# A two-layer transformer kernel on one core: loads by whole rows, Q and K in banks of their own, and a new order of the products

## The chip, the cores and the metric

The kernel runs on one core of a Trainium2 chip. A core has a matrix engine (TensorE, in the profile PE, with PEld for its weight loads), three engines for other arithmetic (VectorE or DVE, ScalarE or ACT, GpSimd or POOL) and a queue engine (SyncE or SP) that issues DMA transfers. TensorE reads its operands from the on-chip memory SBUF and writes into PSUM, here eight banks of 128 partitions by 512 float32; DVE and ACT copy ("evict") results out of a bank before it is used again.

The metric is the device time of one execution in microseconds (us): the median of 3 runs.

## The reference, cut to what matters

The computation is attention with a recurrent memory (A), then a gated feed-forward network (B), and both again with the same weights:

```python
# x: 2048 x 576; 32 heads of 128; 8 memory rows; segments of 32 rows
def A(x, mem0, Wq, Wk, Wv, Wo):
    mem = mem0
    for s in range(64):
        xs = x[32 * s:32 * s + 32]
        h = concat(mem, xs)                      # 40 rows
        q, k, v = h @ Wq, h @ Wk, h @ Wv         # per head
        p = softmax(masked(q @ k.T * 128 ** -0.5))
        o = sum over heads of (p @ v) @ Wo
        mem, out_s = o[:8], o[8:]                # memory goes to the next segment
def B(x, w1, w3, w2):                            # 576 -> 4608 -> 576
    return (silu(x @ w1) * (x @ w3)) @ w2

x = x + A(layernorm(x)); x = x + B(layernorm(x))
x = x + A(layernorm(x)); x = x + B(layernorm(x))
```

(Written out in short form; inputs are bfloat16.) The memory makes the 64 segments of a layer a chain. The kernel therefore walks 72 steps: step t does segment t of the first layer and segment t - 8 of the second one together, where both exist. 576 is 4 x 128 + 64, so every product over Dm has four blocks of 128 rows and a remainder of 64 rows.

## The kernel before: the parts concerned

The kernel builds a list of nodes (a block of products, an eviction, a load), and places them with a small planner. The order of TensorE's nodes is not planned: it is given as a string of letters.

```python
KINDS = {"m0tr": "m", "L0tr": "a", "L1tr": "b", "POST": "p", "Ftr": "n", "QK": "Q", "QKt": "q", "SC": "S", "TR": "T", "PV": "P",
         "WO": "O", "WOt": "o", "VX": "X", "VXt": "x", "VM": "V", "VMt": "v", "FF": "F", "FFt": "f", "VG": "G", "VGt": "g", "W2": "W", "W2b": "w"}
...
ORDER = FIRST + FOUR * 11 + LAST
```

Q is a block of QK products for four heads, q its 64-row remainder; S scores, T the transposed product of the softmax, P its product with V, O and o the products with Wo, X, V and G the V products (small letters their remainders), F, f, W and w the feed-forward network. FOUR is the order of four steps, repeated eleven times.

The loads of the input weights, all on the SP queue:

```python
    def load_qk(self, half):
        def f(n):
            for kind, wd in ((0, self.a.wq), (1, self.a.wk)):
                for c in range(4):
                    w, d = (v.rearrange("p (r h n) -> p r h n", r=2, h=2)[:, :, half] for v in (self.T.W[:, 4 * kind + c, :], wd[c * P:(c + 1) * P, :]))
                    self.dma(w, d)
...
    def load_qkt(self):
        def f(n):
            for kind, wd in ((0, self.a.wq), (1, self.a.wk)):
                self.dma(self.T.W[:, 8, kind * 2048:(kind + 1) * 2048], wd[4 * P:D, :].rearrange("p (r n) -> r p n", r=2))
...
    def load_vt(self):
        return lambda n: self.dma(self.wv(True), self.a.wv[4 * P:D, :].rearrange("p (r n) -> r p n", r=2))
```

A remainder is folded: its 64 rows fill partitions 0 to 63 with the first half of the heads and partitions 64 to 127 with the second, so that two products of 64 rows run side by side in the two halves of the array (the "row" tiling mode).

The QK block and its remainder for unit u (four heads), into two banks:

```python
            for j in range(4):
                h0 = self.head(u // 2, 4 * (u % 2) + j) * E
                for kind in (0, 1):
                    at = (2 * kind + j % 2) * SW
                    for c in range(4):
                        self.mm(self.bk(b[j // 2])[:, at:at + q1 - q0], self.T.W[:, 4 * kind + c, h0:h0 + E], HTt[:, c, q0:q1],
                                first and j % 2 == 0 and kind == 0 and c == 0, c == 3)
...
            for i in (0, 1):
                for kind in (0, 1):
                    at = (2 * kind + i) * SW
                    h0 = (H // 2 * kind + 2 * u + i) * E
                    for r in (0, 1):
                        rr = slice(r * R64, (r + 1) * R64)
                        self.mm(self.bk(b[r])[:, at:at + q1 - q0], self.T.W[rr, 8, h0:h0 + E], HTt[rr, 4, q0:q1],
                                first and i == 0 and kind == 0, True, tile_position=(r * R64, 0))
```

Bank b[0] holds Q and K of the first two heads, b[1] those of the other two. Each bank is evicted by one node, in two copies where both layers are present.

The products with Wo accumulate in a bank that is set apart (YB), while all others come from a pool of seven. After the last Wo product of a step, four small nodes carry the result on: an ACT copy of the new memory columns into HT, an ACT copy of the odd part (YO), a DVE addition for the memory's remainder, and the copies for the residual (YTS).

Of the kernel before, what the change touches and what calls it, by code (L numbers as in the profile page):

```python
# [13 lines left out]
P = 128  # L14
R64 = 64
# [20 lines left out]
POOLS = {"bank": 7, "y": 1, "qkt": 4, "sme": 2, "pb": 2, "pts": 1, "ot": 4,  # L36
# [148 lines left out]
def ewh(*ns):  # L185
# [5 lines left out]
    "amQQqqqqSqQQqSqQQQTQqSSXxvVPTPTOPOTOoooPOoQqqqQQSqqqQQSQQTSVqvqPTQOPSoTOXPToxPOOooaQqqqQQSqQVvSqqQQQqSQqTSPTPOTO"  # L191
    "PTOPoooOoQQqqVSqqvQQQSqQqqqQSTQPTSXPOTOPTxooPOOooQqqqpQvqSVQnQFfqSQQFqqfQQfqSTFSPWTFPOoTOPfoTFPOOooWQfqqQQSqqQQS"
    "qfqQFTFfvVWSQqPQTFqffFSxPOTWPXfFTOPOOooooWQFqqfQFSfqqQQQSqqWTQQFqfvVSqfQFFPSfTWPOTOafPFTOPFOoooofWQQqqvfqSFVQWQq"
    "QSqqQTQPqqSQbOTSXxPXTOPTooPOOooxQQpqqVSqqvQnQQFSfqFTfqQPQqqfSFQTOPSWTOPFOTFPffoooOoWQQqqqQSgqfFQGWQTqSPQFqfqQQSq"
    "fFGTFggfSGPOTOPGfgTOPFOooooWQqqqQQFSffqFaQWQQSqqqQqfFTQWvSVFPTfSOPFfTOPfWOTFPFOooooWQqqfQQSfqqFQWQQqqSqqQbQTGggS"
    "PGTGPSggOTGPOTOPoooOoQqqvppQQSqVqqnQnQFTSfqPQQfqqSFTQPOfoSFOTWwPFffTFPOOooowFfqQWQFqffFWSqQwQgqqGTQSPQqqfFQWGTQg"
    "qSOPFSogfGwTOPFgfGaTOPWOoooFQqqfQwQSqqVqvQQQSfqqQTFPFfqSQWTwPFOfoSTOPwWFffOTFPWwOoooFfqqQQWqqSQQQSqqQbwQTGSqgGPg"
    "TOPQqggoSGTGPOTOPooOo"
)
FOUR = (  # L200
    "qqQpQqqpQQnvVSSqnQFQfqfFTQqqSQPFTffSFPOTOwPWTOPFOoooowQqfqQFSqqfQQWQSqgqQTGwFPSffFGQqqgQTOPWTFSgfgGGPOTOPwOFWffo"
    "oooFQQqqVSvwFfqqQQWTQfqqSFPQwWFqqfSQQTWFPffSFaOwTFPOTOPWOwooooffFQQqqWQSqqqQQQbSqqQTGgqQPSSgGTGPOTggGPOTwPOOoooo"
)
LAST = (
    "QQpvqqVSpQQqqQnqQnSqffTFPFTOQoSfqqQFPFSfTOPwWOFTffFPwOWoooFfqqQQWSwQQgqqGTQPSqqQQQqgqSGTFPOTSfgfGFPOWTwFffgGOPFO"
    "ooooWwQqfqFQQfqqSQFwvVSTWFqfqQQPQqfqSQFTOSowPWTOPFffFTOWPwOoooFqqfQQQSqqqQQQqvvSVSVTWQqPQqTOoSPTOPwOTbPooxOoXqqQ"
    "QppQvqVSqqQQnnQSfqFTQFPSqfqQFTwfSWPOFTOPffTOPFwOooooWQQqqQqfqSFQFfqSQwTQvqfVSWFQFqqfQWSPwTOPFTOPffTFPOWOoooowFqf"
    "qQQQSxqfXFQFfqqQWwSQTFfqVvSWFPTwQqfqQPOToSfPFOwTOPWOoooFfqqQQQqqvSVQQSqWQTqqqSQQPTwSPObOToXPToxPOOooQQpvqqVSqqQQ"
    "QqnQSqqfFQFqfTQPSwSTFPOFTffoPOTOPwOoooFQqfqQQSfqqFQQSqvVqTQwQSqfFPQTOqfPFSoXTFPfxOTOPwOoooFQqqfQQSqqVvQQSqfFTQqQ"
    "SfqqFPQwTOSoPFTFffPOTOPwOoooFQqqQQSfqqQwQvSVqQqfFTSqQPQTfqOPSwTOPfooFTFPOOoopwnFfffFFFwffFFwffFFwffFFwffFFwffFFw"  # L210
# [12 lines left out]
def make_nodes(em, nseg, pools, o=Opt, dma_bw=230e3, load_bw=400e3):  # L223
# [23 lines left out]
    def load(name, nbytes, prio, fn, deps=()):  # L247
# [3 lines left out]
    ld_h = [[load("ldqk", kb(512, 4096), -9.0, em.load_qk(0)), load("ldqt", kb(64, 8192), -8.5, em.load_qkt())],  # L251
            [load("ldqk", kb(512, 4096), -8.0, em.load_qk(1))]]
    ld_v = [load("ldv", kb(512, 4096), -7.0, em.load_v()), load("ldvt", kb(64, 4096), -6.5, em.load_vt())]
# [91 lines left out]
    def step(t):  # L345
# [15 lines left out]
        y = Slot("y", users=2)  # L361
        wos, wots = [], []
        for g in range(NG):
            qs, qe = [], []
            for u in (2 * g, 2 * g + 1):
                q = Slot("qkt", users=1)
                b = banks()
                pq = t + o.qk + o.ustep * u
                m_ = node("PE", 32 * mm80, em.qk(t, u, b), deps=hx + hm[:1] + (ld_h[u // 4] if t == 0 else []),
                          prio=pq, mode="full", acq=[q] + b, name="QK")  # L370
                n = node("PE", 4 * mm80, em.qk_tail(t, u, b), deps=hx + hm + (ld_h[u // 4] if t == 0 else []), prio=pq + o.qkt, mode="row",
                         acq=[q] + b, name="QKt")
                rd += [m_, n]
                me[f"QK{u}"], me[f"QKt{u}"] = m_, n
                for r in (0, 1):
                    qe.append(node("AD", ew(256, 64) if nl == 2 else ew(160), em.qk_ev(t, u, r, q, b[r]), deps=[m_, n], prio=t + o.ustep * u,
                                   rel=[b[r]], name="QKe"))
                qs.append(q)
# [38 lines left out]
        if t == nst - 1:  # L417
            last_reads[1].extend(me[f"{k}{u}"] for u in range(8) for k in ("QK", "QKt"))
# [22 lines left out]
    last_reads = [], []  # L441
    kept = {}

    def job(j):
# [18 lines left out]
        if last:  # L463
            v_done, qk_done = last_reads
            tail = []
            for i in range(8):
                if i == 2:
                    parts = [(0, 9 * 512, v_done), (1, 4 * 576, qk_done)]
                else:
                    parts = [(None, 9 * 512 + 4 * 576, v_done if i < 2 else qk_done)]  # L470
                tail.append([load("tail", kb(128, c), s0 + o.tail_at + 0.01 * i, em.tail_load(i, what), deps=dep) for what, c, dep in parts])
# [89 lines left out]
class Emitter:  # L561


    def __init__(self, nc, tc, T, aps, nseg):
        self.nc, self.tc, self.T, self.nseg = nc, tc, T, nseg
        self.a = aps
        self.last = {}
        self.order_dep = mybir.DependencyInfo(mybir.DependencyClass.NoSync, mybir.DependencyReason.SCHED_ONLY)
        self.tail_w = {}
# [71 lines left out]
    def load_qk(self, half):  # L641
        def f(n):
            for kind, wd in ((0, self.a.wq), (1, self.a.wk)):
                for c in range(4):
                    w, d = (v.rearrange("p (r h n) -> p r h n", r=2, h=2)[:, :, half] for v in (self.T.W[:, 4 * kind + c, :], wd[c * P:(c + 1) * P, :]))
                    self.dma(w, d)
        return f

    def load_qkt(self):

        def f(n):
            for kind, wd in ((0, self.a.wq), (1, self.a.wk)):
                self.dma(self.T.W[:, 8, kind * 2048:(kind + 1) * 2048], wd[4 * P:D, :].rearrange("p (r n) -> r p n", r=2))
        return f
# [11 lines left out]

    def load_vt(self):
        return lambda n: self.dma(self.wv(True), self.a.wv[4 * P:D, :].rearrange("p (r n) -> r p n", r=2))
# [106 lines left out]
    def ln_tr(self, xn, b, warm=False):  # L775

        def f(n):
            for _ in range(10 if warm else 0):
                self.mm(self.T.YB[:], self.T.ident[:, 0:P], self.T.WO[:, 0, 0:512], True, True)
            for c in range(5):  # L780
                self.mm(self.lnps(b)[:, c, :], self.T.XN[:, xn.i, c * P:(c + 1) * P], self.T.ident[:, 0:P], True, True, is_transpose=True)
        return f
# [102 lines left out]
    def head(self, g, j):  # L885

        u, i = 2 * g + j // 4, j % 4
        return H // 2 * (i // 2) + 2 * u + i % 2

    def qk(self, t, u, b):  # L890

        def f(n):
            q0, q1 = self.qcols(t)
            HTt = self.ht(t)
            first = self.begin(b)
            for j in range(4):
                h0 = self.head(u // 2, 4 * (u % 2) + j) * E
                for kind in (0, 1):
                    at = (2 * kind + j % 2) * SW
                    for c in range(4):  # L900
                        self.mm(self.bk(b[j // 2])[:, at:at + q1 - q0], self.T.W[:, 4 * kind + c, h0:h0 + E], HTt[:, c, q0:q1],
                                first and j % 2 == 0 and kind == 0 and c == 0, c == 3)
        return f

    def qk_tail(self, t, u, b):
        def f(n):
            q0, q1 = self.qcols(t)
            HTt = self.ht(t)
            first = self.begin(b)
            for i in (0, 1):  # L910
                for kind in (0, 1):
                    at = (2 * kind + i) * SW
                    h0 = (H // 2 * kind + 2 * u + i) * E
                    for r in (0, 1):
                        rr = slice(r * R64, (r + 1) * R64)
                        self.mm(self.bk(b[r])[:, at:at + q1 - q0], self.T.W[rr, 8, h0:h0 + E], HTt[rr, 4, q0:q1],
                                first and i == 0 and kind == 0, True, tile_position=(r * R64, 0))
        return f

    def qk_ev(self, t, u, r, q, b):  # L920

        def f(n):
            src = self.bk(b)[:, 0:4 * SW].rearrange("p (k h n) -> p k h n", k=2, h=2)
            dst = self.T.QKT[:, q.i, :, 2 * r:2 * r + 2, :]
            if not self.both(t):
                self.cp(n, dst[:, :, :, 0:QW], src[:, :, :, 0:QW])
            elif role(t) == 0:
                self.cp(n, dst[:, :, :, 0:64], src[:, :, :, 16:SW])
                self.cp(n, dst[:, :, :, 64:SW], src[:, :, :, 0:16])
            else:  # L930
                self.cp(n, dst[:, :, :, 32:SW], src[:, :, :, 0:48])
                self.cp(n, dst[:, :, :, 0:32], src[:, :, :, 48:SW])
# [107 lines left out]
    def yT(self, t):  # L1040
        nq = self.nq(t)
        return self.T.YB[:, 0:5 * nq].rearrange("p (c q) -> p c q", c=5), nq
# [154 lines left out]
def kernel(  # L1197
# [65 lines left out]
    T.YB = pp.tile([P, 512], F32, name="YB")  # L1263
# [60 lines left out]
```

## Time and profile before

| what | value |
|---|---|
| runs | 2745.57, 2750.65, 2752.44 us; median 2750.65 |
| span of the profiled execution | 2751.5 us, granted TensorE clock 0.992 |
| PEld, ACT, POOL busy | 2234.0, 1362.0, 333.2 us |
| DMA moved | 321.41 MB, mean 117 GB/s |
| four-step pattern in mid-kernel | 159.2 us |

The page gives busy time of each engine, the span in 40 slices, the DMA queues, the chain of work that ended last, and groups of instructions. A line of the timeline reads: start us, duration us, engine, line of the source, operation, output<-inputs, partitions*columns of the operand, shape, count of merged instructions, and in brackets the idle time before it and what ended it. In the windows, "(x74)" is the number of instructions that began in the stretch, the clock is the granted share, and the DMA share is the mean busy share of 16 DMA engines. Product records are pipelined and overlap: one takes about 200 ns, but the next starts long before it ends, so the distance of the starts is what a product costs.

### The profile page before, as it was taken

What the parts mean: (1) busy time and instruction counts of PE and PEld (TensorE: products, weight loads), DVE (VectorE), ACT (ScalarE), POOL (GpSimd) and SP (SyncE); (2) the same over time, 40 slices, a digit from 0 to 9 for tenths busy, and PEclk for the clock granted to TensorE, in tenths of its full rate; (3) what the DMA queues carried; (4) which work ended last, traced back from release to release, by engine and by line L of the source; (5) the groups of instructions that cost most, each with busy time, mean ns of one, the idle gap of its engine ahead of it and who ended that gap; (6) DMA issues with size and microseconds to landing.
All of it is one profiled execution on the core that took longest, in us unless ns stands there. A gap on an engine that the chain in (4) does not pass through costs nothing.

```text
span 2751.5 us, 126617 instructions
## 1 busy us (share of the span) xinstructions
PE 2657.0 (97%) x55783; PEld 2234.0 (81%) x55783; DVE 2137.9 (78%) x5480; ACT 1362.0 (49%) x3920; POOL 333.2 (12%) x400
## 2 busy tenths in 40 slices
PE   2899999999999999999999999999999999999998
PEld 1688888888888888888888888888888888888886
DVE  2687887787878788787878878787787877787776
ACT  1555554454545455454545545454454545454553
POOL 0111111110101111010111101010110101011110
PEclk8899999999999999999999999999999999999999
DMA  6244534334242433424343342424334342435368
GB/s 226 87 115 131 152 94 132 112 91 131 80 123 78 123 100 106 140 73 122 86 116 106 108 130 80 127 82 116 104 108 123 89 132 72 126 89 149 91 176 246
DMA packets 484863, 321.41 MB, mean 117 GB/s; under 512 B 26350, under 2 KB 476790, under 8 KB 483798
## 3 DMA queue, kind: packets, MB, share of 16 engines
q1 hardware_dynamic: 481126, 306.22, 38.0%
q8 instruction: 436, 7.14, 1.1%
q0 software_dynamic: 3024, 6.93, 0.9%
q14 instruction: 117, 0.96, 0.1%
q10 hardware_dynamic: 160, 0.16, 0.0%
HBM read 308.49 MB, written 2.36 MB: 113 GB/s over the span
## 4 chain that ended last, share of the span: by engine, by line
PE 91%; DVE 3%; ACT 2%; DMA 2%; issue 1%; SPq 1%; POOL 0%; DVEq 0%; ACTq 0%
PE bank L580 79%; PE YB L580 13%; ACT V L583 1%; DMA WV<-in_A_Wv_dram 1%; SPq L589 1%; DVE V L586 1%; DVE STAT L586 1%; DVE SME L586 1%; DMA W<-in_A_Wk_dram 1%; DVE XR L586 0%; ACT SME L583 0%; DMA W<-in_A_Wq_dram 0%; DVE PB L586 0%; DMA W<-in_B_w_dram 0%; ACT HT L583 0%
## 5 line engine op out<-in xcount | busy, mean ns | idle before, releaser
L580 PEld LDWEIGHTS <-W 128*128 128x128 bf16 (+1 forms) x29400 | 1234.3, 98 | 176.6 <-issue 57.1
L580 PE MATMUL bank<-HT,W 128*128 128x80 bf16 (+3 forms) x23040 | 820.4, 197 | 46.8 <-DMA W<-in_A_Wk_dram 19.2
L580 PE MATMUL bank<-XTB,W 128*128 128x256 bf16 (+3 forms) x6360 | 652.3, 262 | 2.2 <-ACT XTB L583 1.4
L583 ACT ACTIVATE QKT<-bank 128x256 bf16<-128x256 f32 (+2 forms) x1533 | 373.5, 307 | 361.7 <-PE bank L580 339.3
L1002 POOL MEMSET PB<- 128x1024 bf16 x288 | 273.9, 951 | 1908.2 <-PE bank L580 1246.9
L580 PE MATMUL YB<-OT,WO 128*128 128x80 bf16 (+3 forms) x11520 | 409.6, 198 | 5.0 <-issue 4.6
L580 PEld LDWEIGHTS <-WO 128*128 128x128 bf16 (+1 forms) x11520 | 378.8, 102 | 19.4 <-issue 12.9
L583 ACT ACTIVATE V<-bank 32x512 bf16<-32x512 f32 (+1 forms) x560 | 318.4, 585 | 144.6 <-PE bank L580 139.3
L580 PE MATMUL bank<-WV,HT 128*32 128x512 bf16 (+4 forms) x3240 | 369.8, 385 | 13.0 <-DMA WV<-in_A_Wv_dram 13.0
L580 PE MATMUL bank<-W2C,HTT 128*128 128x288 bf16 x2240 | 320.5, 288 | 0.0
L583 ACT ACTIVATE HTT<-bank 128x512 bf16<-128x512 f32 (+1 forms) x324 | 177.7, 549 | 261.4 <-PE bank L580 259.8
L586 DVE TENSOR_REDUCE STAT<-SME 104x8 f32<-104x320 f32 (+1 forms) x576 | 275.6, 478 | 21.4 <-ACT SME L583 14.8
L586 DVE TENSOR_TENSOR PB<-SME,STAT 40x128 bf16<-40x128 f32 (+4 forms) x912 | 275.7, 336 | 15.0 <-DVE STAT L586 0.5
L586 DVE SCALAR_TENSOR_TENSOR XR<-bank,XR 128x288 f32<-128x288 f32 x576 | 243.6, 450 | 49.5 <-PE bank L580 42.0
L580 PEld LDWEIGHTS <-HT 128*32 128x32 bf16 (+4 forms) x3240 | 138.4, 96 | 160.9 <-issue 39.9
L580 PEld LDWEIGHTS <-HTT 128*128 128x128 bf16 x2304 | 210.4, 98 | 55.1 <-issue 2.5
L583 ACT ACTIVATE OT<-bank 128x320 bf16<-128x320 f32 (+1 forms) x403 | 150.5, 404 | 183.1 <-PE bank L580 180.6
L586 DVE SCALAR_TENSOR_TENSOR HTT<-HTT,bank 128x512 bf16<-128x512 bf16 (+1 forms) x324 | 201.4, 622 | 43.9 <-ACT HTT L583 41.5
L586 DVE CAST V<-bank 64x512 bf16<-64x512 f32 (+1 forms) x304 | 208.1, 685 | 34.0 <-PE bank L580 27.9
L586 DVE TENSOR_TENSOR HTT<-HTT,bank 128x512 bf16<-128x512 bf16 (+1 forms) x324 | 203.6, 629 | 30.0 <-PE bank L580 0.5
L586 DVE CAST QKT<-bank 128x128 bf16<-128x128 f32 (+4 forms) x515 | 141.5, 316 | 105.3 <-PE bank L580 102.4
L583 ACT ACTIVATE PTS<-bank 128x320 bf16<-128x320 f32 (+1 forms) x379 | 143.3, 404 | 109.2 <-PE bank L580 84.1
(64 smaller groups left out, 1793.1 us busy)
## 6 DMA issues: line engine op xcount, KB each, us to landing
W<-in_B_w_dram SPq DMA_DIRECT2D x612, 256.0 KB, 3.5
W2C<-in_B_w_dram SPq DMA_DIRECT2D x306, 288.0 KB, 3.3
W<-in_B_w_dram SPq DMA_DIRECT2D x612, 32.0 KB, 3.3
W<-in_B_w_dram SPq DMA_DIRECT2D x10, 512.0 KB, 9.3
W<-in_A_Wq_dram SPq DMA_DIRECT2D x9, 512.0 KB, 16.1
W<-in_A_Wk_dram SPq DMA_DIRECT2D x9, 512.0 KB, 9.0
WO<-in_A_Wo_dram SPq DMA_DIRECT2D x8, 576.0 KB, 9.5
XR<-in_A_x_dram POOLq DMA_DIRECT2D x16, 288.0 KB, 2.8
```

What stands on the lines that cost most here:

```text
L580: self.ch("PE", self.nc.tensor.matmul(out, lhsT=lhsT, rhs=rhs, start=start, stop=stop, skip_group_check=True, **k))
L583: self.ch("ACT", self.nc.scalar.activation(*a, **k))
L586: self.ch("DVE", getattr(self.nc.vector, fn_)(*a, **k))
L589: self.ch("SP", self.nc.sync.dma_start(out=out, in_=in_))
L1002: return lambda n: self.ch("POOL", self.nc.gpsimd.memset(self.T.PB[:, pb.i], 0.0))
```

## The change

Six things are changed.

- **Loads.** Q and K are loaded by whole rows (8192 bytes a row) instead of half rows, first all of Wq, then all of Wk. The 64-row remainders are no longer folded: Q's fill partitions 0 to 63 and K's partitions 64 to 127, in one plain DMA each. They go first, half of them on the ACT queue.
- **Banks of Q and K.** Q of four heads goes to b[0], K to b[1]; the pair of remainder products that runs side by side is now Q's and K's of one head.
- **Extra products.** Before the first QK block, six products of 128x512 run on each of the first three blocks of Wk, as they arrive; their results are overwritten.
- **Wo's bank** comes from the pool, which grows from seven to eight banks. It is held from a step's first Wo product to its last copy.
- **Order.** The strings FIRST, FOUR and LAST are new.
- **Last loads.** In the plan, the last loads of feed-forward weights follow Wo's products of the last step one by one, instead of all following QK.

```diff
-POOLS = {"bank": 7, "y": 1, "qkt": 4, "sme": 2, "pb": 2, "pts": 1, "ot": 4,
+POOLS = {"bank": 8, "qkt": 4, "sme": 2, "pb": 2, "pts": 1, "ot": 4,
...
-    "qqQpQqqpQQnvVSSqnQFQfqfFTQqqSQPFTffSFPOTOwPWTOPFOoooowQqfqQFSqqfQQWQSqgqQTGwFPSffFGQqqgQTOPWTFSgfgGGPOTOPwOFWffo"
-    "oooFQQqqVSvwFfqqQQWTQfqqSFPQwWFqqfSQQTWFPffSFaOwTFPOTOPWOwooooffFQQqqWQSqqqQQQbSqqQTGgqQPSSgGTGPOTggGPOTwPOOoooo"
+    "QqqvpQQpQqqVnSSqQnQFfqfFTQqqSQPFffSTFOPwTWOPFTOPWOfooooFwQqqfQQqqSWQQqqgSQwTGFPSffFGQqgqQTOPFTSfggGGPOTOPWwOoooo"
+    "FfqfFQwWFQqfqQQqfvVSSFFQfqqQWTawPFqfqSQQTWOwffoSFPFTOPwTOPWOoooFfqqQQWQqqSQQqqSbQQqqgGTQPSSgGTGPOggTGPOTwPOOoooo"
...
-    ld_h = [[load("ldqk", kb(512, 4096), -9.0, em.load_qk(0)), load("ldqt", kb(64, 8192), -8.5, em.load_qkt())],
-            [load("ldqk", kb(512, 4096), -8.0, em.load_qk(1))]]
+    ld_t = [node("ACT", 0.2, em.load_tail(1), prio=-80, name="ldt", lat=8.0), load("ldt", kb(R64, 6144), -20, em.load_tail(0))]
+    ld_qk = [load("ldqk", kb(512, 4096), kind - 9.0, em.load_qk(kind)) for kind in (0, 1)] + ld_t
...
-        y = Slot("y", users=2)
+        y = em.ys[t] = Slot("bank", users=2)
...
-                    parts = [(None, 9 * 512 + 4 * 576, v_done if i < 2 else qk_done)]
+                    parts = [(None, 9 * 512 + 4 * 576, v_done if i < 2 else qk_done + wo_done[max(i - 4, 0):i - 3])]
...
+    def load_qk(self, kind):
+        def f(n):
+            wd = (self.a.wq, self.a.wk)[kind]
+            for c in range(4):
+                self.dma(self.T.W[:, 4 * kind + c, :], wd[c * P:(c + 1) * P, :])
+        return f
+
+    def load_tail(self, r):
+
+        def f(n):
+            go, wd, rr = ((self.dma, self.a.wq), (self.adma, self.a.wk))[r] + (slice(r * R64, (r + 1) * R64),)
+            go(self.T.W[rr, 8, :], wd[4 * P:D, :])
+            go(self.wv(True)[rr, :], self.a.wv[4 * P:D, r * 2048:(r + 1) * 2048])
         return f
...
+            for c in range(3 if t == u == 0 else 0):
+                for _ in range(6):
+                    self.mm(self.bk(b[1])[:], self.T.ident[:, 0:P], self.T.W[:, 4 + c, 0:512], True, True)
+            for j in range(4):
+                h0 = self.head(u // 2, 4 * (u % 2) + j) * E
+                for kind in (0, 1):
+                    for c in range(4):
+                        self.mm(self.bk(b[kind])[:, j * SW:j * SW + q1 - q0], self.T.W[:, 4 * kind + c, h0:h0 + E], HTt[:, c, q0:q1],
+                                first and j == 0 and c == 0, c == 3)
...
+                    rr = slice(kind * R64, (kind + 1) * R64)
+                    self.mm(self.bk(b[kind])[:, j * SW:j * SW + q1 - q0], self.T.W[rr, 8, h0:h0 + E], HTt[rr, 4, q0:q1],
+                            first and j == 0, True, tile_position=(kind * R64, 0))
```

## The prediction

> **What bounds the kernel now.** I read the page first: engine totals, then the 40 slices.
>
> ```profile
> PE 2657.0 (97%) x55783; PEld 2234.0 (81%) x55783; DVE 2137.9 (78%) x5480; ACT 1362.0 (49%) x3920; POOL 333.2 (12%) x400
> ...
> PE   2899999999999999999999999999999999999998
> ```
>
> TensorE is busy 97% of 2751.5 us. Slices are 68.8 us wide; only the first (2 tenths) and the second (8) are poor. So I asked for the middle and the start separately. First, busy time of each engine in one repeat of the four-step pattern in mid-kernel (columns: window, its length, busy us of PE, PEld, DVE, ACT, POOL, clock, DMA share, GB/s):
>
> ```profile
> 1035.30:1194.50 159.20, 158.24 (x3138) 133.08 (x3132) 127.30 (x321) 80.04 (x230) 18.58 (x23) 1.00 0.37 107
> ```
>
> The repeat takes 159.2 us and PE idles 1 us of it, at full clock. From the start times of successive product records, a 128x80 QK product follows the last after 36 ns and a 128x256 FFN product after 109 ns. The change issues the same products except for 18 more, so the middle has a floor it cannot leave: whatever is gained there is gained from that 1 us. The timeline shows where it goes, once a repeat:
>
> ```profile
> 1033.82 1.69 PE L580 MATMUL YB<-OT,WO 128*128 128x80 bf16 x55
> ...
> 1035.57 0.22 ACT L583 ACTIVATE HT<-YB 128x64 bf16<-128x64 f32 x1 [0.79 <-PE YB L580]
> ...
> 1036.08 0.36 DVE L586 TENSOR_TENSOR HT<-YB,YO 64x16 bf16<-64x16 f32 x2 [2.02 <-ACT YO L583]
> 1036.30 1.47 PE L580 MATMUL bank<-HT,W 64*128 64x80 bf16 x36 [0.80 <-DVE HT L586]
> ```
>
> The step's last Wo products end, and the next PE work in the order is a 64-row QK remainder, which needs the new memory columns through ACT, ACT and DVE: 0.80 us idle (1.00 us from start to start). At another seam a whole QK block comes first, and needs only the first ACT copy:
>
> ```profile
> 398.69 0.48 PE L580 MATMUL bank<-HT,W 128*128 128x80 bf16 x9 [0.34 <-ACT HT L583]
> ```
>
> Then the start. The waits of PE (us in total, times, longest):
>
> ```profile
> PE bank L580 <- DMA W<-in_A_Wk_dram: 19.2, 7, 12.8
> PE bank L580 <- DMA WV<-in_A_Wv_dram: 13.0, 3, 9.4
> ...
> PE bank L580 <- DMA W<-in_A_Wq_dram: 8.4, 1, 8.4
> ```
>
> 40.6 of PE's 94 idle us wait for the three input weights. The timeline tells which part of them:
>
> ```profile
> 26.24 0.21 PE L580 MATMUL bank<-HT,W 64*128 64x40 bf16 x2 [8.36 <-DMA W<-in_A_Wq_dram]
> ...
> 39.30 0.96 PE L580 MATMUL bank<-HT,W 64*128 64x40 bf16 x30 [12.84 <-DMA W<-in_A_Wk_dram]
> ...
> 70.91 3.99 PE L580 MATMUL bank<-WV,HT 64*32 64x512 bf16 x48 [9.39 <-DMA WV<-in_A_Wv_dram]
> ```
>
> The long waits all end at products with 64 rows: the remainders, rows 512 to 575 of Dm. Last, the DMA in five stretches (same columns as above):
>
> ```profile
> 7.00:15.00 8.00, 1.69 (x17) 1.17 (x17) 3.17 (x12) 2.24 (x5) 0.56 (x1) 1.00 1.00 373
> 15.00:23.00 8.00, 2.08 (x57) 1.96 (x57) 0.00 (x0) 0.00 (x0) 0.00 (x0) 1.00 0.13 55
> 47.00:51.00 4.00, 1.24 (x32) 1.12 (x32) 0.00 (x0) 0.43 (x2) 0.00 (x0) 0.50 1.02 424
> 63.00:67.00 4.00, 0.00 (x0) 0.00 (x0) 0.00 (x0) 0.00 (x0) 0.00 (x0) 0.50 0.13 53
> 71.00:79.00 8.00, 6.03 (x104) 3.06 (x104) 6.43 (x12) 6.10 (x14) 1.47 (x2) 0.71 0.99 306
> ```
>
> 373 GB/s while the half-row pieces (2 KB) come, 424 with whole rows (8 KB), 306 with Wo's 1152-byte pieces, and 53 to 55 GB/s at a share of 0.13 while a remainder comes alone. 0.13 is 2 engines of 16.
>
> **What the skill says.** The Trainium skill, "DMA: Bandwidth & Descriptors", Rules for kernel authors: an outermost dimension of size c below 16 confines the whole DMA to at most c engines. The remainders are loaded as "r p n" with r = 2 outermost; the 0.13 agrees. The same page, Issuing engines are not separate DMA queues: a second issuing engine saves only issue time; so I count the ACT queue's share of the remainders as order, not bandwidth (no run yet shows it). "TensorE: Matmul & The Clock Gate", What's actually happening: the clock is halved after an idle window of about 3.4 us and comes back after as long a busy one. The trace agrees: 0.50 at 63 to 67 us, where PE does nothing. "PSUM — Partial Sum Buffer", PSUM bank collisions raise a hardware error: two row tiles may not write one bank at once; that is why each of the paired remainders needs its own bank, before (two head pairs) as after (Q and K). No time follows from it.
>
> **The change, part by part.**
>
> *Loads.* Wq, Wk and Wv are 576 x 4096 x 2 B = 4.72 MB each, 14.16 MB; now the last of it lands at 70.9 us. After: every DMA has 64 or 128 rows outermost, so all 16 engines. The first 10 us moved 250 GB/s in the trace before (2.5 MB, start included); I keep that, and put the rest at 400 GB/s, a little under the 424 of whole rows. Order: remainders (1.57 MB), Wq, Wk, Wv. Wk complete: 9.96 + 0.15 MB of x, less 2.5, is 7.6 MB or 19 us: 29 us. Wv: 11.8 MB or 29.5 us: 39.5 us. Wo (4.72 MB at 306) takes 15.4 us: 55 us.
>
> *Step 0 on PE.* The first QK block now needs all of Q and K. From 29 us: 256 products at 35 ns (89 took 3.15 us in the timeline) and 64 remainders at about 18 ns make 10.3 us: 39.3 us, just when Wv lands. From the last Wv landing to the next step's first QK it took 85.25 - 70.91 = 14.3 us before; 39.5 + 14.3 = 53.8. Wo's last group lands at 55, and its products and the seam need 2 us more: 57. I take the later, 57. Gain: 85.2 - 57 = **28 us**, nearly all on the path, as PE is the bound from there on.
>
> *Extra products.* 18 of 128x512 at 427 ns, the gap of such products at half clock in the last job's warm-up, are 7.7 us. They run while Wk's last three blocks of 1 MB arrive (3 x 2.6 us): **0**. They keep PE from idling and may spare some halved stretches; before, 0.50 was granted in 46.9-53.7, 60.5-74.2, 77.6-81.0, 87.8-91.2 and 101.5-104.9 us. Those after 77 us total 10 us of small products whose gap hardly depends on the clock: **-1 us**.
>
> *Seam.* The new pattern begins with a whole QK block, not remainders: 1.00 to 0.54 us (the gap at 398 us), 12 times: **-5.5 us**.
>
> *Tiling mode changes.* Walking the letters, PE changes between full, row and column tiling 1429 times before and 1452 after. A full QK product just after a row-tiled one starts 131 ns after it, not 36: 23 x 0.095 = **+2 us**.
>
> *Q and K in separate banks.* Same products and the same bytes evicted. But a bank of two heads was complete halfway through the block; now both complete at its end. In one place per repeat only about 0.6 us of PE work lies between a QK block and the scores that need it; two ACT evictions (386 and 227 ns) plus latency do not fit. I allow 0.25 us, 12 times: **+3 us**.
>
> *Wo's bank from the pool, last loads.* The waits list no PE wait for a free bank worth counting, so the eighth bank is worth about **0**. The order of the last FFN loads on the queue is the same in both kernels, with no added wait; and from 2690 to 2730 us DMA is full (share 1.03 to 1.09 in stretches of 10 us), so PE cannot hurry ahead there: **0**.
>
> Sum: -28 - 1 - 5.5 + 2 + 3 = -29.5 us: 2721 us. I round to 2720.
>
> **Rivals.**
> (1) Loads slower than 400 GB/s: 44 to 46 us ran at 329 with a share of 1.01. Then Wv lands at 46 and Wo at 61; the second step starts at 63, gain 22: 2726. Against it: those 2 us mixed half-row and whole-row pieces.
> (2) Waiting for all of Q and K puts QK itself on the path: PE idles until about 29 us where it began at 12.8. At 329 GB/s Wk is complete at 33 and QK ends at 43.5, still before Wv's 46. It costs only if QK runs at half clock; with 5 us more, 2725.
> (3) A new stall in the repeated pattern: each microsecond costs 12. DVE is at 80% of a repeat, so a group moved too near its softmax would do it. The distances between producers and users that I compared in the two orders are alike, softmax to transposed product 5.8 us of PE work in both: not expected, 2732 if so.
> (4) The new order also removes the gaps of steps 1 to 4 (PE idles 6.3 us between 100 and 200 us; a new order may fill them): 2714.
>
> **Range and chances.** The load term is certain in sign and good to 8 us; the pattern's terms repeat 12 times and are good to perhaps 10 us. 8 times in 10: 2704 to 2734. Faster by 2% would be under 2696, needing (4) and more: 0.07. Slower by 2% needs a pattern 7 us longer per repeat: 0.01.
>
> **What would show it.** No stretch at share 0.13 in the first 60 us; Wv's last product wait ending near 40 us; the second step's QK starting near 57; a repeat of 158.5 to 159.5 us. It is wrong if the second step starts after 70 us, if the repeat moves by over 1 us, or if PE begins to wait for the last FFN loads.

## The result, and the profile after

| | median us | lowest to highest | runs |
|---|---|---|---|
| before | 2751.55 | 2745.57 to 2752.79 | 4 |
| after | 2708.74 | 2706.62 to 2711.45 | 4 |

The ratio is 0.9849, 95% interval 0.9832 to 0.9866: 1.5% faster, within 2%, and inside the predicted range. The gain is 42.8 us where about 31 were predicted: the time is 11 us below the predicted 2720, and the trace tells where. This is the page after, its engine totals and PE's 40 slices of 67.7 us:

```profile
PE 2646.6 (98%) x55801; PEld 2229.8 (82%) x55801; DVE 2104.6 (78%) x5431; ACT 1376.0 (51%) x3970; POOL 332.9 (12%) x400
...
PE   5999999999999999999999999999999999999998
```

PE's idle time fell from 94 to 61 us, and the first slice rose from 2 tenths to 5. But busy time fell too, by 10 us, with 18 more products. In part this can be the clock: half speed was granted for 47.7 us of the trace before and for 11.7 us of the trace after. Another part can be stops that do not show as idle time: product records last about 200 ns and overlap, so that a shorter stop still counts as busy. To find the places I took from both traces the time at which each step ends (the start of the ACT copy of Wo's odd part, YO, seventy-two of them; step 0 is the first):

| stretch | before us | after us | difference | predicted |
|---|---|---|---|---|
| start to the end of step 0 | 85.23 | 61.94 | -23.3 | -28 |
| to the end of step 16 | 509.49 | 505.74 | -3.7 | -1 and a share of the next row |
| ten repeats of four steps, 16 to 56 | 1591.74 | 1582.02 | -9.7 | -0.4 (12 repeats: -0.5) |
| steps 57 to 60 | 164.52 | 157.09 | -7.4 | 0 |
| steps 61 to 70 | 328.77 | 328.38 | -0.4 | 0 |
| step 71, the last | 30.22 | 24.33 | -5.9 | 0 |
| after the last step | 41.57 | 47.81 | +6.2 | 0 |

Steps 57 to 60 and the end must be read together. By the new order 48 feed-forward products (544 before, 496 after) leave steps 57 to 60: 12 of them now come earlier, 28 in steps 61 to 70 and 8 in the last step. At about 0.12 us each (the distance of the starts of such products) that is 5.8 of the 7.4 us: work moved, not saved. In exchange 36 smaller ones, of 128 columns, leave steps 61 to 71 and come after the last step; their starts are 56 ns apart, so they are 2.0 us.

**The start.** PE's waits in the whole trace after:

```profile
PE bank L581 <- DMA W<-in_A_Wk_dram: 12.5, 2, 11.7
...
PE bank L581 <- DMA W<-in_B_w_dram: 5.9, 5, 1.7
PE bank L581 <- issue: 5.7, 5, 2.8
```

The 40.6 us of waits for Wq, Wk and Wv have become 12.5; no wait for Wv is left. Two smaller items stand in the list: waits for feed-forward weights, and time in which PE stood still though nothing in the profile held it ("issue"). The DMA in the start (columns as in the prediction):

```profile
7.00:15.00 8.00, 0.93 (x10) 0.76 (x11) 3.65 (x13) 2.24 (x5) 0.56 (x1) 1.00 1.00 329
15.00:23.00 8.00, 0.00 (x0) 0.00 (x0) 0.00 (x0) 0.00 (x0) 0.00 (x0) 1.00 1.02 425
23.00:31.00 8.00, 6.77 (x30) 2.67 (x30) 0.00 (x0) 0.00 (x0) 0.00 (x0) 1.00 1.01 422
...
39.00:47.00 8.00, 4.75 (x137) 3.43 (x136) 4.68 (x14) 1.75 (x7) 0.00 (x0) 0.90 1.07 387
47.00:55.00 8.00, 5.72 (x102) 2.79 (x94) 7.29 (x17) 6.52 (x14) 1.90 (x2) 0.89 1.11 362
```

No stretch at 0.13 is left: all engines are at work from 7 us on, as the Trainium skill ("DMA: Bandwidth & Descriptors", Rules for kernel authors) let one expect once the outermost dimension is 64 or 128. PE's timeline in step 0 (start, duration, and in brackets the idle time before):

```profile
23.41 6.47 PE L581 MATMUL bank<-W,ident 128*128 128x512 bf16 x18 [11.69 <-DMA W<-in_A_Wk_dram]
...
30.87 2.00 PE L581 MATMUL bank<-HT,W 128*128 128x40 bf16 x73 [0.82 <-DMA W<-in_A_Wk_dram]
...
37.71 1.09 PE L581 MATMUL bank<-HT,W 128*128 128x40 bf16 x37 [1.12 <-issue]
...
44.18 0.49 PE L581 MATMUL bank<-HT,W 128*128 128x40 bf16 x13 [2.80 <-issue]
...
45.48 5.89 PE L581 MATMUL bank<-WV,HT 64*32 64x512 bf16 x80
...
61.96 2.06 PE L581 MATMUL bank<-HT,W 128*128 128x40 bf16 x80 [0.32 <-ACT HT L584]
```

Wk is complete at 30.9 us, close to the 29 predicted, and Wv at 41.8 (its last piece was issued at 20.9 and took 20.9 us to land), predicted 39.5. But the QK products, which should have taken 10.3 us, end only at 45.5: 3.9 us of it is idle time put down to issue. V then starts at half clock, with groups of four products about 427 ns apart until 48.6, against 217 ns after. The second step begins at 61.96, not at 57.

**The repeat.** The same stretch as in the prediction, one repeat between two seams:

```profile
1004.45:1162.62 158.17, 157.60 (x3136) 132.91 (x3132) 124.02 (x316) 82.09 (x235) 18.52 (x23) 1.00 0.37 107
```

158.17 us, against 159.16 in nearly every repeat before: -0.99, ten times over. Most of it, 0.64 us, came out of PE's busy time (158.24 to 157.60) and not out of its listed idle time. The seam, in the timeline, is as predicted:

```profile
1003.32 1.36 PE L581 MATMUL bank<-OT,WO 128*128 128x80 bf16 x46
...
1004.75 0.23 ACT L584 ACTIVATE HT<-bank 128x64 bf16<-128x64 f32 x1 [0.79 <-PE bank L581]
...
1005.03 1.70 PE L581 MATMUL bank<-HT,W 128*128 128x80 bf16 x48 [0.34 <-ACT HT L584]
```

A whole QK block follows after the first ACT copy: 0.34 us idle, 0.54 from start to start, where it was 0.80 and 1.00. That is 0.46 of the 0.99 us.

**The end.** PE's idle times in the last step and behind it, before:

```profile
2686.18 0.58 PE L580 MATMUL bank<-HT,W 128*128 128x40 bf16 x17 [1.73 <-issue]
...
2702.28 0.19 PE L580 MATMUL YB<-OT,WO 128*128 128x40 bf16 x1 [1.17 <-issue]
2708.85 1.05 PE L580 MATMUL YB<-OT,WO 128*128 128x40 bf16 x30 [2.04 <-issue]
```

And after, where the last step ends at 2659.5:

```profile
2686.22 2.36 PE L581 MATMUL bank<-XTB,W 64*128 64x128 bf16 x36 [1.07 <-DMA W<-in_B_w_dram]
2691.51 2.36 PE L581 MATMUL bank<-XTB,W 64*128 64x128 bf16 x36 [1.74 <-DMA W<-in_B_w_dram]
2696.76 3.97 PE L581 MATMUL bank<-XTB,W 64*128 64x128 bf16 x40 [1.68 <-DMA W<-in_B_w_dram]
```

4.9 us of issue idles leave the last step; 4.5 us of waits for weights come behind it, with the 36 products more (2.0 us). Against them stands that the stretch begins at full clock: the ten microseconds from 2710 ran at 0.70 before, those from 2660 at 1.00 after.

### The profile page after: what moved, and what is told of

Its sections match the earlier page's. It is cut to its first block, busy times and chain, and to the rows that moved or that the text cites. A ratio compares the mean times of both kernels' runs of the same rounds, so it can differ in the third digit from the quotient of the medians.

```text
span 2707.3 us, 126684 instructions
## 1 busy us (share of the span) xinstructions
PE 2646.6 (98%) x55801; PEld 2229.8 (82%) x55801; DVE 2104.6 (78%) x5431; ACT 1376.0 (51%) x3970; POOL 332.9 (12%) x400
## 4 chain that ended last, share of the span: by engine, by line
PE 90%; DVE 4%; DMA 3%; ACT 2%; issue 1%; SPq 0%; POOL 0%; ACTq 0%; DVEq 0%
PE bank L581 90%; DMA W<-in_B_w_dram 1%; ACT V L584 1%; DVE STAT L587 1%; DVE SME L587 1%; DMA W<-in_A_Wk_dram 1%; DVE HTT L587 1%; DVE PB L587 1%; DVE V L587 1%; DMA WV<-in_A_Wv_dram 0%; DVE PTS L587 0%; ACT QKT L584 0%; DMA W2C<-in_B_w_dram 0%; SPq L590 0%; ACT HT L584 0%
## 5 line engine op out<-in xcount | busy, mean ns | idle before, releaser
L581 PE MATMUL bank<-HT,W 128*128 128x80 bf16 (+3 forms) x23040 | 809.4, 196 | 11.9 <-ACT HT L584 6.2
L584 ACT ACTIVATE QKT<-bank 128x256 bf16<-128x256 f32 (+4 forms) x1555 | 366.0, 307 | 406.3 <-PE bank L581 392.3
L581 PE MATMUL bank<-OT,WO 128*128 128x80 bf16 (+2 forms) x11520 | 409.4, 198 | 1.8 <-DVE OT L587 0.7
L584 ACT ACTIVATE V<-bank 64x512 bf16<-64x512 f32 (+1 forms) x605 | 342.1, 585 | 123.4 <-PE bank L581 117.0
L584 ACT ACTIVATE SME<-SME 104x320 f32<-104x320 f32 (+1 forms) x288 | 135.5, 470 | 175.4 <-DVE SME L587 171.9
L587 DVE CAST QKT<-bank 128x128 bf16<-128x128 f32 (+2 forms) x493 | 136.3, 317 | 105.9 <-PE bank L581 102.9
L584 ACT ACTIVATE OT<-bank 128x320 bf16<-128x320 f32 (+1 forms) x382 | 144.3, 405 | 141.9 <-PE bank L581 138.7
L587 DVE CAST V<-bank 64x512 bf16<-64x512 f32 (+1 forms) x259 | 177.2, 684 | 40.1 <-PE bank L581 34.5
```

The source lines that it names most:

```text
L581: self.ch("PE", self.nc.tensor.matmul(out, lhsT=lhsT, rhs=rhs, start=start, stop=stop, skip_group_check=True, **k))
L584: self.ch("ACT", self.nc.scalar.activation(*a, **k))
L587: self.ch("DVE", getattr(self.nc.vector, fn_)(*a, **k))
```

## The experiments

Each is compared with runs of the kernel before on the same chip; "repeat" is the commonest distance of two steps four apart between steps 16 and 56 (37 distances in each trace).

**1 and 2. The loads alone.** The kernel before, with the folded remainders each loaded as two DMAs of 64 rows:

```diff
-                self.dma(self.T.W[:, 8, kind * 2048:(kind + 1) * 2048], wd[4 * P:D, :].rearrange("p (r n) -> r p n", r=2))
+                for r in (0, 1):
+                    self.dma(self.T.W[r * R64:(r + 1) * R64, 8, kind * 2048:(kind + 1) * 2048], wd[4 * P:D, r * 2048:(r + 1) * 2048])
```

(and Wv's likewise).

> The kernel before, with one thing changed: each folded 64-row remainder of Wq, Wk and Wv is loaded by two DMAs of 64 rows instead of one with an outermost dimension of 2. Order of the products, banks and half-row loads stay. Theory (the two-engine remainders are the cause of the slow start): no stretch at a DMA share of 0.13, the first step ends near 62 us instead of 85, and the time is 2751.5 - 23 = 2728 us. Rival (whole rows, the early position of the remainders and the new order carry the start): the first step ends after 72 us and the time is 2740 us or more.

Measured 2725.39 us, ratio 0.9914 (0.9896 to 0.9932). The DMA in two stretches that stood at a share of 0.13 and 0.72 before:

```profile
15.00:23.00 8.00, 4.44 (x117) 3.82 (x118) 1.05 (x4) 0.50 (x2) 0.00 (x0) 1.00 1.03 271
...
31.00:39.00 8.00, 6.11 (x169) 5.33 (x170) 4.10 (x12) 2.56 (x9) 0.95 (x1) 0.72 1.02 421
```

Step 0 ends at 63.60, -21.6, and from step 7 on the trace stays 24.3 us ahead. The repeat is unchanged, 159.18. So the number of engines that a remainder is spread over is nearly the whole start. Then Wq and Wk by whole rows, one after the other, as well:

```diff
-            for kind, wd in ((0, self.a.wq), (1, self.a.wk)):
-                for c in range(4):
-                    w, d = (v.rearrange("p (r h n) -> p r h n", r=2, h=2)[:, :, half] for v in (self.T.W[:, 4 * kind + c, :], wd[c * P:(c + 1) * P, :]))
-                    self.dma(w, d)
+            wd = (self.a.wq, self.a.wk)[half]
+            for c in range(4):
+                self.dma(self.T.W[:, 4 * half + c, :], wd[c * P:(c + 1) * P, :])
```

> As the one before, and Wq and Wk also by whole rows, all of Wq and then all of Wk. Theory (whole rows only bring the last Wv row a little earlier, and PE catches up on QK before that): within 3 us of the run with the remainders alone, about 2727 us. Rival (waiting for all of Q and K puts QK on the path): 5 us slower, 2733 us, with the first step ending 5 us later.

Measured 2723.70 us, 0.9905 (0.9890 to 0.9919): the interval overlaps that of run 1. The 1.7 us between the medians cannot be told from nothing.

**3. The extra products.** The kernel after with `range(0)` for the three blocks, so 18 products fewer, whose results are not used.

> The kernel after without the 18 extra products in step 0. Theory (they only fill time in which PE waits for Wk's blocks): 2708.7 us, within 2. Rival (they keep the TensorE clock up, and QK and V of step 0 run at half clock without them): 3 to 5 us slower, 2712 to 2714 us, with a granted clock near 0.5 between 30 and 45 us.

2710.23 us, 0.9857 (0.9842 to 0.9872), against 0.9849 for the kernel after: no difference that can be told. Step 0 ends 1.2 us later in the trace.

**4 and 5. The order.** The kernel after with the strings of before, and the kernel before with the strings of after:

```diff
 FIRST = ( ... )   # all three strings exchanged
 FOUR = ( ... )
 LAST = ( ... )
```

> The kernel after (its loads, its banks for Q and K, Wo's bank from the pool) with the three order strings of the kernel before. Theory (beyond the start, the order alone brings the gain): the start's 24 to 26 us stay, one four-step repeat takes 159.2 us again, and the time is 2749.7 - 25 = 2725 us. Rival (the separate banks of Q and K end the waits inside the 64-row remainders, 0.58 us a repeat): a repeat of 158.6 us and 2718 us.

Measured 2717.38 us, 0.9886 (0.9871 to 0.9901), repeat 158.55: the rival's number. The theory gave the order all of the gain in the middle; here it has 0.38 of 0.99 us.

> The kernel before (its loads, its banks, Wo's bank apart) with the order strings of the kernel after. Theory (the order alone): the slow start stays, a repeat takes 158.2 us, the stretch from the last repeat to the end gains 5 to 7 us as after, and the time is 2749.7 - 18 = 2732 us. Rival (the new order needs the new banks): a repeat of 159 us or more, with PE waits on QKT or on evictions, and 2745 us or more.

Measured 2739.89 us, 0.9962 (0.9948 to 0.9977), repeat 158.63. So the order brings 0.53 us in the kernel before (159.16 to 158.63) and 0.38 in the kernel after (158.55 to 158.17); the seam's 0.46 lies between. About half a microsecond in each repeat is left for the banks, and I put it down to Q and K. The next two runs tested that.

**6 and 7. Which banks?** The kernel after with Wo's bank apart again:

```diff
-POOLS = {"bank": 8, "qkt": 4, ...
+POOLS = {"bank": 7, "y": 1, "qkt": 4, ...
-        y = em.ys[t] = Slot("bank", users=2)
+        y = em.ys[t] = Slot("y", users=2)
-        return self.bk(self.ys[t])[:, 0:5 * nq].rearrange("p (c q) -> p c q", c=5), nq
+        return self.T.YB[:, 0:5 * nq].rearrange("p (c q) -> p c q", c=5), nq
```

> The changed kernel, but Wo's product keeps a PSUM bank of its own as before the change, beside a pool of seven. The two runs with exchanged orders left some 0.56 us in each repeat of four steps for the banks, which could be the separate banks of Q and K or the eighth bank of the pool. Theory (it is Q and K in separate banks, since the waits that vanished stood inside the 64-row remainders; the eighth bank is worth nothing): repeat 158.2 us, total 2708 to 2711. Rival (it is the eighth bank, a bank more in hand for every product that waits for one): repeat 158.6 to 158.8, total 2714 to 2718.

2721.39 us, 0.9889 (0.9873 to 0.9906): 11 us slower than the kernel after by the two ratios. My theory fell, and by more than the rival said. And the other way round, the pool's bank and the new order with Q and K of two heads in one bank (run 2's kernel with the new strings and):

```diff
-POOLS = {"bank": 7, "y": 1, "qkt": 4, ...
+POOLS = {"bank": 8, "qkt": 4, ...
-        y = Slot("y", users=2)
+        y = em.ys[t] = Slot("bank", users=2)
-        return self.T.YB[:, 0:5 * nq].rearrange("p (c q) -> p c q", c=5), nq
+        return self.bk(self.ys[t])[:, 0:5 * nq].rearrange("p (c q) -> p c q", c=5), nq
```

> The changed kernel's order, 64-row remainders in two transfers, whole rows of Wq and Wk and Wo's bank from the pool, but Q and K of a pair of heads in one bank as before the change, no extra products, and the remainders' transfers on the old queue. Theory (separate banks bring 0.56 us in each repeat): repeat 158.7 to 158.8 us, with waits of 0.2 to 0.35 us back inside the 64-row remainders, total 2715 to 2718. Rival (the banks carry nothing, the pool's eighth bank does): repeat 158.2, total 2708 to 2711.

2710.14 us, 0.9854 (0.9838 to 0.9869), again the rival's number. One repeat of each, first with Wo's bank apart:

```profile
1047.12:1206.03 158.91, 158.16 (x3129) 133.16 (x3127) 125.10 (x317) 81.00 (x236) 18.56 (x22) 1.00 0.37 107
```

and with the old banks of Q and K:

```profile
727.33:885.48 158.15, 157.59 (x3129) 132.95 (x3127) 123.94 (x317) 82.65 (x235) 18.56 (x22) 1.00 0.37 107
```

All six repeats together, in us:

| Wo's bank | Q and K | old order | new order |
|---|---|---|---|
| apart | two heads a bank | 159.16 (before) | 158.63 |
| apart | separate | not run | 158.91 |
| from the pool | two heads a bank | not run | 158.15 |
| from the pool | separate | 158.55 | 158.17 (after) |

With the new order, the pool's bank brings 0.48 us with the old banks of Q and K and 0.74 with separate ones. Separate banks cost 0.28 us with seven banks in the pool, and nothing (0.02) with eight.

Run 6 is worse than its commonest repeat says. Only 17 of its 37 distances are 158.90 to 158.94 us; others reach 159.55 (in one of these PE waits 0.37 us for feed-forward weights, at 1510 us). The mean of the ten repeats from step 16 to 56 is 159.17 before, 158.69 in run 5, 159.14 in run 6, 158.27 in run 7 and 158.20 after. By these means the pool's bank brings 0.42 and 0.94 us, and separate banks cost 0.45 with seven banks. Twelve times 0.94 is the 11 us of the total.

Where it lies can be seen, since the kernel after and that of run 6 give PE the same products in the same order. I laid a repeat of each side by side, block of products by block. Run 6 falls behind in four places, by 0.17, 0.34, 0.07 and 0.12 us, and nowhere else by over 0.06. Run 7, laid beside the kernel after in the same way, falls behind nowhere by over 0.06. This is the largest place, first in the kernel after:

```profile
999.47 0.49 DVE L587 CAST OT<-bank 128x320 bf16<-128x320 f32 x1
...
999.98 0.45 PE L581 MATMUL bank<-ident,PB 104*128 104x80 bf16 x8
...
1000.26 1.15 PE L581 MATMUL bank<-W2C,HTT 128*128 128x288 bf16 x8
```

and with Wo's bank apart:

```profile
1163.31 0.45 PE L581 MATMUL bank<-ident,PB 104*128 104x80 bf16 x8
1163.39 0.49 DVE L587 CAST OT<-bank 128x320 bf16<-128x320 f32 x1
...
1163.93 1.14 PE L581 MATMUL bank<-W2C,HTT 128*128 128x288 bf16 x8 [0.17 <-DVE OT L587]
```

The W2 products read W2C and HTT, not OT. By elimination, what they wait for is the bank that the copy to OT empties: 0.62 us from the start of the products with PB, where it takes 0.28 with eight banks in the pool. The profile's list of waits shows 0.17 of these 0.34 us, and of the smaller places nothing.

Laid beside run 5, which has the same order and seven banks too but Q and K two heads to a bank, run 6 loses most at remainder products of the feed-forward network (0.17 us) and of QK (0.12). Those are two of the same four places, and with eight banks they lose nothing: so they too wait for a bank. The scores, which read the evicted Q and K, take longer at one place in the repeat, 0.80 us in place of 0.76, with seven banks and with eight.

**8 and 9. The end.** The kernel after without the last feed-forward loads of blocks 3 to 7 (a part of block 2's stays); the products then read whatever lies in SBUF, so these runs leave transfers out:

```diff
-            if what != 1:
+            if what != 1 and i < 3:
...
-            if what != 0:
+            if what != 0 and i < 3:
```

> The kernel after without the last loads of feed-forward weights (blocks 3 to 7 and the W2 half of block 2 are left out of... only blocks 3 to 7 are left out; their products read what lies in that space, so the work on PE is the same). Theory (the end now waits for DMA): PE's waits for feed-forward weights, 4.5 us in the last 45 us, are gone, and the time is 2703 to 2705 us. Rival (PE would have waited for something else): within 1.5 us of 2708.7.

2708.16 us, 0.9850 (0.9836 to 0.9865). The waits for weights are gone, and what follows the last step shrinks from 47.8 to 43.0 us. But one new idle takes it all back inside the last step (step 70 to 71: 28.0 us, not 24.3):

```profile
2663.10 0.41 PE L581 MATMUL bank<-OT,WO 128*128 128x40 bf16 x7 [2.51 <-issue]
```

The same edit on the kernel before:

> The kernel before without the same last loads (blocks 3 to 7; the products read what lies there). Theory (PE waits for its own instructions where DMA is full): of the three idle times that end by nothing the profile shows, 1.7 us at 2684, 1.2 at 2701 and 2.0 at 2706, the last falls away or shrinks under 0.7 us, since the last loads fill the DMA engines there, and the time is 2 to 4 us less, 2746 to 2748 us. Rival (another cause): the idle times stay as they are, and so does the time, 2749.7 us.

2748.73 us, 0.9996 (0.9988 to 1.0005); the idles remain (1.30 and 2.32 us). It tells little: the loads of the first three blocks still filled the DMA engines there (share 1.04 to 1.10 between 2690 and 2710).

**10. The last loads on another queue.** The kernel after, blocks 3 to 7 issued by GpSimd instead of SyncE:

```diff
+            go = self.swdma if i >= 3 else self.dma
-                    self.dma(t13[:, 4 * kind:4 * kind + 4], ...
+                    go(t13[:, 4 * kind:4 * kind + 4], ...
```

> The changed kernel, but the last FFN loads from the fourth block on are issued from GpSimd's queue and not from SyncE's, where they stand behind the stores of the last step. Theory (TensorE waits for these loads after the last step because they were issued 3.7 us after its end; issued when their space is free, they land in time): the 4.5 us of waits in the last 50 us go, total 2703 to 2705. Rival (the loads then fill the DMA engines during the last step, and TensorE stands idle there with nothing released, 2 to 5 us, as it does in the kernel before): total 2707 to 2710, with idles of over 1 us put down to issue between 2635 and 2665.

2712.14 us, 0.9861 (0.9846 to 0.9875): no gain, though the waits for these weights shrink to 2.4 us. The first of these loads was issued 3.9 us after the end of the last step, as late as on SyncE (3.7), because GpSimd's own work stood ahead of it: until 2668.06 it waited for a layer norm's input from DVE. The run doesn't answer what earlier loads would bring.

**11 and 12. What are the issue idles?** In all fourteen traces PE has 44 idles of 0.9 us or more that are put down to issue. Every one of them ends 1.23 to 1.60 us after the end of a 16 KB packet of the DMA queue that the page calls "q8 instruction". In the kernel after the packets follow each other every 3.3 to 10.9 us (median 5.8), so chance would have scattered the idles over all of that. And in the four microseconds ahead of each idle the DMA share was 0.52 to 1.14, in all but five of them over 0.8. In the kernel after the packets begin at 35.34, 41.61 and 47.94 us, 6.3 us apart; once the loads are through (63.75, 68.58, 72.08, 75.53) mostly 3.5. So I suspected that PE runs out of instructions, since their packets come late where the engines are full. First, Wo's loads held back until the last QK eviction of step 0, by a small copy out of it ahead of them on the queue:

```diff
+                    for l in ld_o:
+                        l.after(*qe[-2:])
...
+                self.dma(self.T.HOLD[:], self.T.QKT[:, self.hold_q.i, 0, 0, 0:16])
```

> The kernel after, with Wo's loads held back until the last QK eviction of step 0 (a small copy out of that eviction's tile goes ahead of them on the queue). In the trace after, PE idles 2.8 us at 41.2 to 44.2 us and 1.1 us at 36.4, released by nothing that the profile shows, each time about 1.3 us after a 16 KB instruction packet ended. Theory (PE waits for its own instructions, whose fetch is late while DMA is full): the idle time at 41 to 44 us falls under 1.5 us, as the DMA engines run empty at about 40 us, and the time is 2706 to 2708 us, for Wo comes later but still in time for its groups. Rival (another cause): the idle time stays at 2.8 us, and the time is 2709 to 2713 us, because Wo comes later.

2713.22 us, 0.9867 (0.9852 to 0.9882); the idle of 2.80 us stays. That is the rival's number, but the run doesn't decide: I had overlooked that Wv's own transfers keep the engines full until 42.5 us, and the packet behind the idle began at 42.47. So, with Wv's loads held back as well:

```diff
+                    for l in ld_v[:1] + ld_o:
+                        l.after(*qe[-2:])
```

> The changed kernel, but the loads of Wv and Wo start only when the last Q/K eviction of step 0 is done (a small copy of its output stands ahead of them), so that the DMA engines are empty while step 0's Q/K products run, once Wk has landed near 31 us. It tells what the idles of 1.1 and 2.8 us in that stretch are, which end 1.3 to 1.6 us after a 16 KB packet of the instruction queue. Theory (TensorE's instructions come late because their packets share full DMA engines): with the engines empty the packets follow each other 3.5 to 4.4 us apart, no issue idle over 0.3 us remains between 31 us and the end of the Q/K products, and that phase takes 11 to 12.5 us where it took 15.0. The total is 2714 to 2722, since V and Wo now wait for their weights. Rival (the idles have to do with TensorE's own pace or clock and not with the transfers): the phase still takes 14.5 to 15.5 us with idles of over 1 us in it, total 2718 to 2726.

2722.46 us, 0.9893 (0.9878 to 0.9907), slower, as V now waits for its weights, and at the edge of what both had given for the total. The QK stretch tells them apart. The DMA in the QK stretch, in this run:

```profile
37.00:39.00 2.00, 1.32 (x50) 1.21 (x49) 1.12 (x4) 0.50 (x2) 0.00 (x0) 1.00 0.09 24
39.00:41.00 2.00, 1.77 (x75) 1.56 (x72) 1.09 (x3) 0.69 (x3) 0.00 (x0) 1.00 0.03 8
41.00:43.00 2.00, 1.80 (x68) 1.75 (x65) 1.82 (x7) 0.97 (x3) 0.00 (x0) 1.00 0.00 0
```

and in the kernel after:

```profile
39.00:41.00 2.00, 1.77 (x79) 1.60 (x75) 1.74 (x5) 0.89 (x4) 0.00 (x0) 1.00 1.03 391
41.00:43.00 2.00, 0.38 (x16) 0.28 (x11) 0.98 (x4) 0.27 (x1) 0.00 (x0) 1.00 1.08 380
```

PE in this run:

```profile
38.47 1.09 PE L585 MATMUL bank<-HT,W 128*128 128x40 bf16 x37 [0.68 <-issue]
...
40.52 1.95 PE L585 MATMUL bank<-HT,W 64*128 64x40 bf16 x71 [0.23 <-ACT QKT L588]
```

The idle of 2.80 us is gone; the packets begin at 35.70, 39.76 and 43.03. From the last wait for Wk to the first V product it took 11.2 us (32.07 to 43.28), where the kernel after took 14.6 (30.87 to 45.48). The first idle, 0.68 us here, did not go, against the letter of the expectation; the engines were still full until 37 us (share 1.13 from 35 to 37). So full DMA engines make the idles, or at least the long one.

That the instruction packets are the link can be counted. The kernel after has 111,819 instruction records of PE (55,801 products, as many weight loads, 217 others) and 437 packets: 256 instructions to a packet. Its five waits for issue, all 5.7 us of them, stand after 449, 705, 6849, 7105 and 107,969 instructions, each of which is 193 more than a multiple of 256. So are all 44 idles, but for those late in seven traces in which 82 to 84 product records are missing; they stand at 110 to 112 more, as the missing records would have it. So each of these stops stands where one packet is used up and the next begins. In the kernel after the packet for the 2.80 us idle began when PE had no instruction left, and the one for the idle of 1.12 us when it had 77 (the median of all packets is 239); in run 12 the same two packets began with 166 and 140 left.

## Why the prediction was right or wrong

**Right: the kind of bound, and the loads.** The start was the one large term, and it came from the remainders' two engines: runs 1 and 2 are 24 and 26 us faster than the kernel before beside them. Rival (1), slower loads, did not come: Wk and Wv landed within 2.5 us of the prediction. The seam is right to the hundredth (0.54 us), and the extra products are worth nothing that can be told.

**Wrong, step 0 on PE: "256 products at 35 ns ... make 10.3 us", and the second step at 57.** It began at 61.96. The 35 ns is a distance at half clock: the 89 products ran at 49.99 to 53.14 us, inside the stretch of 46.9 to 53.7 at 0.50. In step 0 after, at full clock, they follow each other after 25 ns, so that the 10.3 us should have been 7.6; nor is it so that the gap of such products "hardly depends on the clock". This error hid part of what was missing. Two things were left out. Idle time with full DMA engines, 1.12 and 2.80 us, in which PE's next instructions came late; such idles stood in the trace before (1.15 us at 88.2 us, 4.9 in the last step), and I had not asked what they were. And V at half clock for 3 us after PE had stood still for nearly three. The Trainium skill ("TensorE: Matmul & The Clock Gate", What's actually happening) has the clock halved after an idle window of about 3.4 us. The trace agrees in kind: the clock read 1.00 from 40 to 45 us and 0.71, 0.50, 0.50 and 0.58 in the four microseconds after; but 2.80 us of standing still, among small products, were enough here.

**Wrong, the largest miss: "the eighth bank is worth about 0".** It was read from the list of waits, which has no line for a free bank. Run 6 puts it at 11 us of total time, 0.74 in the commonest repeat and 0.94 in the mean one. The waits were there, but each cost 0.34 us or less, and most of that is not in the list at all.

**Wrong in its place: "separate banks ... +3 us".** The 0.28 us a repeat that they cost with seven banks is close to the 0.25 allowed, but by luck: the allowance was for scores that wait for two late evictions, and the scores lose 0.04 us. The rest of the cost goes away with the eighth bank, with which it is 0.02 in all. I added up the two terms as if they were independent; the one takes the cost of the other away.

**The order.** Seam -0.46 and mode changes +0.17 made -0.29 us a repeat; exchanging the strings gave -0.53 and -0.38, so the mode changes' +0.17 did not show in the sum. Rival (4), gaps in steps 1 to 4, was small: what steps 1 to 16 gained is 3.7 us, with all else in it.

**Wrong, the last loads: "PE cannot hurry ahead there: 0".** PE did come earlier than its weights: it waited 4.5 us for them, which the prediction named as a sign against itself. The new plan of these loads is not the cause: run 7, which keeps the old plan, waits 4.5 us for them as well (1.19, 1.67 and 1.67), and run 4, which has the new plan but the old order, 0.3. It cost little in the sum because the last step lost 4.9 us of idles, of which I had foreseen nothing. They too stand where one packet ends and the next begins. The 2.51 us idle of run 8 and the 2.04 us one of the kernel before stand before the same packet, the one that begins after 110,785 instructions; in the kernel after that packet had ended 1.36 us before its first instruction, just in time. Why it came late again with the loads left out is open.

The repeat moved by 0.99 us, at the edge of the "over 1 us" that I had given as refutation. That the range held is luck in part: against the prediction the start fell 5 us short, and unforeseen gains of 9 us in the ten repeats, 7.5 from step 57 to the end and 3 in steps 1 to 16 outweighed it.

## What to carry to other kernels

That a trace lists no wait for a buffer does not say that another one is worth nothing. Many stops of 0.1 to 0.3 us are not listed as waits; lay two traces of the same order side by side, or build the kernel with one buffer fewer, and see where it falls behind. An idle that nothing released can be placed by counting the engine's instructions up to it and comparing the count with the packets that bring them. When one part of a change needs a resource longer and another gives more of it, they have to be counted together: alone, the separate banks were a loss. And a load whose share of the DMA engines is 2 of 16 is worth asking about before anything else.

## What the runs showed of the hardware that was not expected

PE can stand still for 0.9 to 3.8 us with nothing released to it late, in or just behind stretches of nearly full DMA engines; with them empty (0.00 to 0.09) the same products ran without the 2.80 us idle. Each of the 44 such idles stood at the first instruction of a new 16 KB packet of the instruction queue, 256 instructions long, and ended 1.23 to 1.60 us after that packet had ended; for half of the packets of the kernel after the distance is 4.5 us or more, and it is never under 1.31. In the full stretch of step 0 these packets came 6.3 us apart, and with the engines empty 3.3 to 4.1. The Trainium skill ("DMA: Bandwidth & Descriptors", Queues, rings and completion order) says that each DMA engine serves its queues in turn, a packet at a time, which fits a packet that must wait for others; no run here shows the order in which they were served. The packets themselves took 1.0 to 1.1 us in the full stretch and 0.9 in the empty one, so it is their start that is late.
